# Attention and a feed-forward block in float32: attention on 128-token tiles with the mean on DVE, strips of 512 tokens, another weight conversion

## The chip, the cores and the metric

The kernel runs on one core of a Trainium2 chip. A core has engines that run side by side, each working through its own queue in order: TensorE (PE) for matrix products and transposes, with a second row PEld for loading its stationary operand; VectorE (DVE), ScalarE (ACT) and GpSimd (POOL) for elementwise work; and SyncE (SP), which here issues data transfers (DMAs). TensorE writes its results to PSUM; DVE and ACT take them from there to SBUF, the on-chip memory. The metric is the device time of one execution in microseconds (us), as the median of several runs. A profile is one further execution, recorded by the hardware profiler.

## The reference

Two blocks follow each other. The first is linear attention with a normalization per head, over 8 batches, 8 heads, 576 tokens and 64 features per head, in float32:

```python
kv = np.einsum('bhsd,bhse->bhde', k, v)
out = np.einsum('bhsd,bhde->bhse', q, kv)
rms = np.sqrt(np.mean(out * out, axis=-1, keepdims=True) + 1e-06)
attn = out / rms * g_norm
# x: (B, H, S, D) -> (B*S, H*D), 4608 tokens of 512 features
h = x @ w_in              # 512 -> 2048
r = np.maximum(h, 0.0)
out = (r * r) @ w_out     # 2048 -> 512
```

The two weights arrive as float64, which no engine here computes in. The kernel gets their bits as 64-bit integers and makes float32 of them on the chip. All products are in float32.

## The kernel before, in words

**Attention** runs in 32 units of one batch and two heads (128 features). The 576 tokens of a batch lie as 96 partitions by 6 places. `transpose_q` (L175) brings q's features onto partitions with six transposes of 96 tokens, into two PSUM tiles, copied by DVE and ACT. `key_value` (L188) forms the 128x128 product of k and v in six products, copies the two diagonal blocks (one per head) into a zeroed matrix `kvd`, and issues the loads of the unit three further on. `query` (L202) multiplies: `kvd` is stationary, q transposed streams in two halves of 288 tokens, so the result `x_ps` has features on partitions. ACT squares it. `root` (L213) gets the mean over a head's features, which now lies across partitions, by another product with a block-diagonal matrix `mean_w` of 1/64; then ACT's square root, DVE's reciprocal and a Newton step on DVE and POOL follow, all on 128x288 elements. `normalize` (L232) multiplies `x_ps` by the result and by `g_col` and writes x, already transposed, into `xT`.

**Feed-forward** runs in 12 strips of 384 tokens. `up` (L277) computes 128 of the 2048 inner features for the strip in four products of 384 columns, ACT applies the maximum with zero, DVE squares. `down` (L293) computes 128 tokens by 512 features in 16 products of 512 columns, issued in four parts; DVE or ACT copies the result and SP stores it. A strip has 16 up and 12 down steps.

**Weights** come in 32 pieces of 128x512 (16 of `w_in`, then 16 of `w_out`) through three buffers `raw`. `convert` (L112) splits each word: DVE isolates and clamps the exponent (L119, L123), ACT scales it (L126), DVE joins the sign (L127), masks the upper mantissa (L132), ACT scales that (L136), DVE adds the lower word (L137), and POOL multiplies the two parts (L140). Then the next piece's load is issued.

**The order** is written out by hand: the program's order is each engine's order. Before the first strip come the five slices of each of batch 0's four units, with a piece converted after every second slice up to eight. In strip 0, each step is preceded by one piece (later two), followed by as many slices of later units' attention as the token count asks for. Loads, weight pieces and stores all go through SP's queue in program order; only the first three units' q and the small `g_col` go through ACT's.

Of the kernel before, what the change touches and what calls it, by code (L numbers as in the profile page):

```python
# [14 lines left out]
ALU = mybir.AluOpType  # L15


@with_exitstack
def kernel(
# [27 lines left out]
    TP = S // C  # L47
    HC, HS = C // 2, S // 2
    PAIR = 2 * S  # tokens in one tile of x: two batches
    STRIP = 384  # L50
    NG = STRIP // P
    N_STRIP = n_tok // STRIP
    N_UNIT = B * NP
    AHEAD = 3  # units whose q, k, v are on chip or on their way
    OQ = 4  # pieces that the second product of 128 tokens is issued in
    N_RAW = 3
# [4 lines left out]
    qkv_pool = ctx.enter_context(tc.tile_pool(name="qkv", bufs=AHEAD))  # L61
    qt_pool = ctx.enter_context(tc.tile_pool(name="qt", bufs=3))
    xt_pool = ctx.enter_context(tc.tile_pool(name="xt", bufs=2))
    asb_pool = ctx.enter_context(tc.tile_pool(name="asb", bufs=2))
    raw_pool = ctx.enter_context(tc.tile_pool(name="raw", bufs=N_RAW))
    g_pool = ctx.enter_context(tc.tile_pool(name="g", bufs=FC + 2))
    osb_pool = ctx.enter_context(tc.tile_pool(name="osb", bufs=3))
    apsum = ctx.enter_context(tc.tile_pool(name="apsum", bufs=2, space=bass.MemoryType.PSUM))
    xpsum = ctx.enter_context(tc.tile_pool(name="xpsum", bufs=2, space=bass.MemoryType.PSUM))
# [3 lines left out]
    loaded = {}  # L73

    def load(u, eng):
        b, p = divmod(u, NP)
        hs = slice(2 * p, 2 * p + 2)
        t = {}
        # q and k are stationary operands: both heads' features lie side by side
        for n, src, e in (("q", q, eng), ("k", k, nc.sync)):  # L80
            t[n] = qkv_pool.tile([TP, C, 2, D], FP32, name=n, tag=n)
            for h in range(2):
                e.dma_start(
                    out=t[n][:, :, h, :], in_=src[b, 2 * p + h].rearrange("(sp c) d -> sp c d", c=C)
                )
        t["v"] = qkv_pool.tile([TP, 2, C, D], FP32, name="v", tag="v")
        nc.sync.dma_start(out=t["v"], in_=v[b, hs].rearrange("h (sp c) d -> sp h c d", c=C))
        loaded[u] = t

    for u in range(AHEAD):  # L90
        load(u, nc.scalar)

# [16 lines left out]

    piece_at = [0]  # L110

    def convert(n):  # L112
        while piece_at[0] < min(n, len(pieces)):
            i = piece_at[0]
            low = raw[i].bitcast(U32).rearrange("p (n two) -> p n two", two=2)[:, :, 0]
            high = raw[i].bitcast(I32).rearrange("p (n two) -> p n two", two=2)[:, :, 1]
            # 2 ** exponent with the sign; 0 below float32's normal range, inf above it
            e = asb_pool.tile([P, WN], I32, name="w_e", tag="w_e")
            nc.vector.tensor_scalar(  # L119
                out=e, in0=high, scalar1=20, scalar2=0x7FF,  # L120
                op0=ALU.logical_shift_right, op1=ALU.bitwise_and,
            )
            nc.vector.tensor_scalar(  # L123
                out=e, in0=e, scalar1=E_BIAS, scalar2=E_BIAS + 255, op0=ALU.max, op1=ALU.min
            )
            nc.scalar.activation(e, e, AF.Identity, bias=e_bias, scale=2.0**23)  # L126
            nc.vector.scalar_tensor_tensor(  # L127
                out=e, in0=high, scalar=-(2**31), in1=e, op0=ALU.bitwise_and, op1=ALU.bitwise_or
            )
            # 1 + mantissa: its upper 20 bits, then the lower 32  # L130
            top = asb_pool.tile([P, WN], I32, name="w_top", tag="w_top")
            nc.vector.tensor_scalar(  # L132
                out=top, in0=high, scalar1=0xFFFFF, scalar2=None, op0=ALU.bitwise_and
            )
            m = asb_pool.tile([P, WN], FP32, name="w_m", tag="w_m")
            nc.scalar.activation(m, top, AF.Identity, bias=one, scale=2.0**-20)  # L136
            nc.vector.scalar_tensor_tensor(  # L137
                out=m, in0=low, scalar=2.0**-52, in1=m, op0=ALU.mult, op1=ALU.add
            )
            nc.gpsimd.tensor_tensor(out=pieces[i][1], in0=m, in1=e.bitcast(FP32), op=ALU.mult)  # L140
            load_piece()
            piece_at[0] += 1

    for i in range(N_RAW):
        load_piece()
# [8 lines left out]
    E_BIAS = 1023 - 127  # L154
    e_bias = const.tile([P, 1], FP32, name="e_bias")
    nc.vector.memset(e_bias, -E_BIAS * 2.0**23)
    one = const.tile([P, 1], FP32, name="one")
    nc.vector.memset(one, 1.0)
    eps_t = const.tile([P, 1], FP32, name="eps_t")
    nc.vector.memset(eps_t, EPS)  # L160
    # block-diagonal 1/D: the mean over a head's features, on all its partitions
    mean_w = const.tile([P, P], FP32, name="mean_w")
    nc.vector.memset(mean_w, 0.0)
    nc.vector.memset(mean_w[0:D, 0:D], 1.0 / D)
    nc.vector.memset(mean_w[D:P, D:P], 1.0 / D)
    kvd = []
    for i in range(3):
        t = const.tile([P, P], FP32, name=f"kvd{i}")
        nc.vector.memset(t, 0.0)
        kvd.append(t)  # L170

# [1 line left out]
    qT, x_ps, sq, rms, xt = {}, {}, {}, {}, {}  # L173

    def transpose_q(u):  # L175
        t = qt_pool.tile([P, S], FP32, name="qT", tag="qT")
        qT[u] = t
        by_place = t.rearrange("p (sp c) -> p c sp", c=C)
        for i in range(2):
            ps = apsum.tile([P, HC, TP], FP32, name="t_ps", tag="at")  # L180
            for j in range(HC):
                nc.tensor.transpose(  # L182
                    ps[:, j, :], loaded[u]["q"][:, i * HC + j].rearrange("p h d -> p (h d)"), ident[0:TP, 0:TP]
                )
            cp = nc.scalar.copy if i else nc.vector.tensor_copy
            cp(by_place[:, i * HC : (i + 1) * HC, :], ps)  # L186

    def key_value(u):  # L188
        t = loaded.pop(u)
        ps = apsum.tile([P, P], FP32, name="kv_ps", tag="at")  # L190
        for c in range(C):
            nc.tensor.matmul(  # L192
                ps, lhsT=t["k"][:, c].rearrange("p h d -> p (h d)"), rhs=t["v"][:, :, c, :],
                start=(c == 0), stop=(c == C - 1),
            )
        d = kvd[u % len(kvd)]
        nc.scalar.copy(d[0:D, 0:D], ps[0:D, 0:D])
        nc.vector.tensor_copy(d[D:P, D:P], ps[D:P, D:P])
        if u + AHEAD < N_UNIT:
            load(u + AHEAD, nc.sync)  # L200

    def query(u):  # L202
        for i in range(2):
            ps = xpsum.tile([P, HS], FP32, name="x_ps", tag="x")
            nc.tensor.matmul(  # L205
                ps, lhsT=kvd[u % len(kvd)], rhs=qT[u][:, ts(i, HS)], start=True, stop=True
            )
            s = asb_pool.tile([P, HS], FP32, name="sq", tag="sq")
            nc.scalar.activation(s, ps, AF.Square)  # L209
            x_ps[u, i], sq[u, i] = ps, s  # L210
        del qT[u]

    def root(u):  # L213
        for i in range(2):
            ps = apsum.tile([P, HS], FP32, name="s_ps", tag="at")
            nc.tensor.matmul(ps, lhsT=mean_w, rhs=sq.pop((u, i)), start=True, stop=True)  # L216
            r = asb_pool.tile([P, HS], FP32, name="r_rms", tag="r_rms")
            nc.scalar.activation(r, ps, AF.Sqrt, bias=eps_t)  # L218
            nc.vector.reciprocal(r, r)  # L219
# [6 lines left out]
            nc.gpsimd.tensor_scalar(  # L226
                out=c, in0=c, scalar1=-0.5, scalar2=1.5, op0=ALU.mult, op1=ALU.add
            )
            nc.gpsimd.tensor_tensor(out=r, in0=r, in1=c, op=ALU.mult)  # L229
            rms[u, i] = r  # L230

    def normalize(u):  # L232
# [120 lines left out]
```

## Time and profile before

| quantity | value |
|---|---|
| median of 3 runs | 1269.7 us (1269.4 to 1270.31) |
| span of the profiled execution | 1268.2 us |
| TensorE busy (matmul) | 1150.5 us, 91% |
| weight load (PEld) | 639.3 us, 50% |
| DVE busy | 434.2 us, 34% |
| ACT busy | 230.9 us, 18% |
| POOL busy | 182.1 us, 14% |
| mean granted TensorE clock | 0.946 |
| moved by DMA | 55.14 MB, 43 GB/s over the span |

The span runs from the first to the last instruction of the core; the runs' time has a little more around it. Busy time counts an engine's instructions, overlapping ones once. The granted clock is the share of TensorE's full speed that the throttle let through. A group of instructions is given as line, engine, operation, output and inputs, shape and count, then busy time in us, mean ns of one, and the idle time of its engine just before, with what ended it. In a timeline a row gives start and length in us. A float32 matrix product leaves two matmul records in the trace, a transpose one.

### The profile page before, as it was taken

How to read it: one execution, taken by the hardware profiler on the slowest of the kernel's cores; microseconds unless marked ns; L12 is line 12 of the kernel's file. 1: busy time of each engine (PE TensorE's matmuls, PEld its weight loads, DVE VectorE, ACT ScalarE, POOL GpSimd, SP SyncE). 2: the span in 40 equal slices, each digit the busy share in tenths (PEclk: the TensorE clock that was granted, in tenths of full speed). 3: DMA queues.
4: the chain of work that ended last, by engine and by line, in shares of the span. 5: the costliest groups of instructions: out<-in, count | busy, mean ns of one | idle time of the engine just before them, and what ended most of it. 6: DMA issues, size and time to landing. Idle time of an engine off the chain costs nothing.

```text
span 1268.2 us, 9232 instructions
## 1 busy us (share of the span) xinstructions
PE 1150.5 (91%) x3520; PEld 639.3 (50%) x3520; DVE 434.2 (34%) x641; ACT 230.9 (18%) x462; POOL 182.1 (14%) x230
## 2 busy tenths in 40 slices
PE   4456645799999999999999999999999999999998
PEld 3244322356456456455465465465465565454553
DVE  3667776433233234124133233143142232220110
ACT  2323323212012112012021021021021121020110
POOL 1333232211111111101011111111011111100000
PEclk8557768899999999999999999999999999999999
DMA  8332423111111111011110111110010000000000
GB/s 215 113 106 84 127 83 111 36 45 38 36 37 28 45 37 29 26 37 28 36 42 23 44 37 29 45 32 23 35 28 9 17 1 9 17 0 17 9 0 25
DMA packets 92429, 55.14 MB, mean 43 GB/s; under 512 B 77536, under 2 KB 83680, under 8 KB 92384
## 3 DMA queue, kind: packets, MB, share of 16 engines
q1 hardware_dynamic: 88672, 53.66, 14.6%
q10 hardware_dynamic: 3712, 0.89, 0.3%
q8 instruction: 28, 0.46, 0.2%
q14 instruction: 17, 0.14, 0.0%
HBM read 45.09 MB, written 9.44 MB: 43 GB/s over the span
## 4 chain that ended last, share of the span: by engine, by line
PE 83%; DVE 10%; ACT 4%; issue 1%; POOL 1%; DMA 1%; ACTq 0%
PE o_ps L298 38%; PE h_ps L281 36%; PE kv_ps L192 3%; PE x_ps L205 2%; PE s_ps L216 2%; DVE w_e L119 2%; ACT w_e L126 2%; ACT w_m L136 2%; DVE w_e L127 2%; DVE w_e L123 2%; PE t_ps L182 1%; DVE r_rms L219 1%; DVE w_top L132 1%; DVE w_m L137 1%; DVE gt L288 1%
## 5 line engine op out<-in xcount | busy, mean ns | idle before, releaser
L281 PE MATMUL h_ps<-xT,w_in 128*128 128x384 f32 x1536 | 515.8, 493 | 0.0
L298 PE MATMUL o_ps<-w_out,gt 128*128 128x512 f32 x1152 | 505.5, 594 | 0.0
L281 PEld LDWEIGHTS h_ps<-xT,w_in 128*128 128x128 f32 x1536 | 294.0, 193 | 196.6 <-issue 11.0
L298 PEld LDWEIGHTS o_ps<-w_out,gt 128*128 128x128 f32 x1152 | 218.1, 191 | 255.1 <-issue 249.0
L288 DVE TENSOR_TENSOR gt<-r 128x384 f32<-128x384 f32 x192 | 109.5, 571 | 306.6 <-ACT r L286 306.6
L286 ACT ACTIVATE r<-h_ps 128x384 f32<-128x384 f32 x192 | 94.0, 489 | 424.8 <-PE h_ps L281 400.6
L225 POOL TENSOR_TENSOR newton<-newton,r_rms 128x288 f32<-128x288 f32 x64 | 54.8, 856 | 753.5 <-DVE newton L222 753.5
L219 DVE RECIPROCAL r_rms<-r_rms 128x288 f32<-128x288 f32 x64 | 124.6, 1947 | 64.3 <-ACT r_rms L218 64.3
L192 PE MATMUL kv_ps<-v,k 96*128 96x128 f32 x384 | 59.5, 315 | 42.7 <-DVE newton L222 42.5
L304 DVE COPY o_sb<-o_ps 128x512 f32<-128x512 f32 x24 | 16.6, 692 | 226.1 <-PE o_ps L298 223.1
L192 PEld LDWEIGHTS kv_ps<-v,k 96*128 96x128 f32 x384 | 57.0, 226 | 55.8 <-DVE newton L222 46.7
L216 PE MATMUL s_ps<-sq,mean_w 128*128 128x288 f32 x128 | 41.9, 452 | 32.5 <-ACT qT L186 32.0
L205 PE MATMUL x_ps<-qT,kvd 128*128 128x288 f32 x128 | 42.0, 456 | 30.5 <-DVE xT L239 30.5
L186 DVE COPY qT<-t_ps 128x288 f32<-128x288 f32 x32 | 21.3, 666 | 129.4 <-PE t_ps L182 129.4
L229 POOL TENSOR_TENSOR r_rms<-r_rms,newton 128x288 f32<-128x288 f32 x64 | 50.8, 794 | 5.3
L216 PEld LDWEIGHTS s_ps<-sq,mean_w 128*128 128x128 f32 x128 | 25.4, 205 | 50.0 <-ACT qT L186 34.9
L205 PEld LDWEIGHTS x_ps<-qT,kvd 128*128 128x128 f32 x128 | 26.3, 211 | 46.5 <-DVE xT L239 32.6
L209 ACT ACTIVATE sq<-x_ps 128x288 f32<-128x288 f32 x64 | 25.8, 410 | 103.2 <-PE x_ps L205 101.4
L218 ACT ACTIVATE r_rms<-s_ps,eps_t 128x288 f32<-128x288 f32 x64 | 31.2, 501 | 63.3 <-PE s_ps L216 62.6
L126 ACT ACTIVATE w_e<-w_e,e_bias 128x512 int32<-128x512 int32 x32 | 23.1, 721 | 82.4 <-DVE w_e L123 82.4
L140 POOL TENSOR_TENSOR w_in<-w_m,w_e 128x512 f32<-128x512 f32 x16 | 22.2, 1389 | 83.8 <-DVE w_m L137 83.8
L304 ACT COPY o_sb<-o_ps 128x512 f32<-128x512 f32 x12 | 7.0, 587 | 143.3 <-PE o_ps L298 136.8
(30 smaller groups left out, 330.4 us busy)
## 6 DMA issues: line engine op xcount, KB each, us to landing
k<-in_k_dram SPq DMA_DIRECT2D x64, 144.0 KB, 3.4
v<-in_v_dram SPq DMA_DIRECT2D x32, 288.0 KB, 3.7
out_dram<-o_sb SPq DMA_DIRECT2D x36, 256.0 KB, 2.0
q<-in_q_dram SPq DMA_DIRECT2D x58, 144.0 KB, 3.1
raw<-in_moe_w_in_dram SPq DMA_DIRECT2D x16, 512.0 KB, 3.6
raw<-in_moe_w_out_dram SPq DMA_DIRECT2D x16, 512.0 KB, 3.3
q<-in_q_dram ACTq DMA_DIRECT2D x6, 144.0 KB, 6.1
g_col<-in_g_norm_dram ACTq DMA_DIRECT2D x2, 0.2 KB, 3.6
```

The lines of the kernel that those rows point to most:

```text
L126: nc.scalar.activation(e, e, AF.Identity, bias=e_bias, scale=2.0**23)
L192: nc.tensor.matmul(ps, lhsT=t["k"][:, c].rearrange("p h d -> p (h d)"), rhs=t["v"][:, :, c, :], start=(c == 0), stop=(c == C - 1),)
L205: nc.tensor.matmul(ps, lhsT=kvd[u % len(kvd)], rhs=qT[u][:, ts(i, HS)], start=True, stop=True)
L216: nc.tensor.matmul(ps, lhsT=mean_w, rhs=sq.pop((u, i)), start=True, stop=True)
L218: nc.scalar.activation(r, ps, AF.Sqrt, bias=eps_t)
L219: nc.vector.reciprocal(r, r)
L225: nc.gpsimd.tensor_tensor(out=c, in0=c, in1=r, op=ALU.mult)
L229: nc.gpsimd.tensor_tensor(out=r, in0=r, in1=c, op=ALU.mult)
L281: nc.tensor.matmul(ps, lhsT=w_in[:, kc, ts(fc, P)], rhs=xt[m][:, kc, t0 : t0 + STRIP], start=(kc == 0), stop=(kc == NP - 1),)
L286: nc.scalar.activation(r, ps, AF.Relu)
L288: nc.vector.tensor_tensor(out=t, in0=r, in1=r, op=ALU.mult)
L298: nc.tensor.matmul(o_ps[0], lhsT=gt[fc][:, ts(g, P)], rhs=w_out[:, fc, :], start=(fc == 0), stop=(fc == FC - 1),)
```

## The change

All three parts are rewritten.

Attention puts tokens on partitions. A batch's 576 tokens are four chunks of 128 and a rest of 64; the rests of two batches form one tile together, so there are nine tiles of 128 tokens per two batches, 36 in all. k, v and q of a unit are loaded by five DMAs for the chunks and three for the rest, all from SP. `transposed_query` has four transposes of 128 tokens and one ACT copy (for odd batches one transpose and one DVE copy more, for the rest tile). `key_value` has five products, and POOL clears the two off-diagonal blocks of a fresh `kvd`. `query` works on one tile of 128 tokens and all 512 features: q transposed is stationary, `kvd` streams, four products (eight of half height for a rest tile). The mean is now along the free dimension: ACT squares, DVE sums by head, and square root, reciprocal and Newton step work on 128x8 elements, all on DVE but the root. DVE scales into `x_n`; `features` transposes the tile on TensorE, and ACT copies with `g_col` into `xT`.

The strips have 512 tokens, four tiles: nine strips of 16 up and 16 down steps. Strip s has its own `xT` tile. A list of slices is worked off evenly over a strip's steps but the last three, up to what the next strip needs.

The conversion clamps the upper word as a float32 (ACT's absolute value, DVE's maximum and minimum), shifts and masks it, joins sign and top exponent bit, and adds the lower word's top bits as an integer: two ACT and four DVE operations, none on POOL. Before strip 0, two pieces are converted; in it, `NP + 2 + 3 * i // 2` up to step i.

The diff, cut to its core:

```diff
-    C = 6  # token s of a batch sits at partition s // C, place s % C
-    STRIP = 384
+    C = S // P
+    REST = S - C * P
+    PAIR = 2 * C + 1
+    NT = 4
+    STRIP = NT * P
...
+        for n, src in (("k", k), ("v", v), ("q", q)):
+            whole = src[b, hs, 0 : C * P].rearrange("h (sp c) d -> sp h c d", c=C)
...
+            nc.sync.dma_start(
+                out=rest[n, b // 2, p][half], in_=src[b, hs, C * P : S].rearrange("h s d -> s h d")
+            )
...
+            nc.scalar.activation(c, high_f, AF.Abs)
             nc.vector.tensor_scalar(
+                out=c, in0=c, scalar1=LEAST, scalar2=MOST, op0=ALU.max, op1=ALU.min
+            )
             nc.vector.tensor_scalar(
+                out=ci, in0=ci, scalar1=3, scalar2=0x3FFFFFFF,
+                op0=ALU.logical_shift_left, op1=ALU.bitwise_and,
+            )
             nc.vector.scalar_tensor_tensor(
+                out=dest, in0=high, scalar=-(2**30), in1=ci, op0=ALU.bitwise_and, op1=ALU.bitwise_or
+            )
+            nc.scalar.activation(r, low, AF.Copy, scale=2.0**-29)
+            nc.vector.tensor_tensor(out=dest, in0=dest, in1=r, op=ALU.add)
...
-            nc.gpsimd.tensor_tensor(out=pieces[i][1], in0=m, in1=e.bitcast(FP32), op=ALU.mult)
...
+    def query(n):
+        m, c = divmod(n, PAIR)
+        ps = apsum.tile([P, d_model], FP32, name="x_ps", tag="at")
...
+                nc.tensor.matmul(o, lhsT=qT[b, p][:, c_b, :], rhs=kvd[b, p], start=True, stop=True)
+        nc.scalar.activation(sq, ps, AF.Square)
+        nc.vector.reduce_sum(out=ms, in_=by_head(sq), axis=AX.X)
+        nc.vector.tensor_scalar(out=ms, in0=ms, scalar1=1.0 / D, scalar2=EPS, op0=ALU.mult, op1=ALU.add)
+        nc.scalar.activation(r, ms, AF.Sqrt)
+        nc.vector.reciprocal(r, r)
+        nc.vector.scalar_tensor_tensor(out=t, in0=ms, scalar=-0.5, in1=r, op0=ALU.mult, op1=ALU.mult)
+        nc.vector.tensor_tensor(out=t, in0=t, in1=r, op=ALU.mult)
+        nc.vector.scalar_tensor_tensor(out=r, in0=t, scalar=1.5, in1=r, op0=ALU.add, op1=ALU.mult)
+        nc.vector.tensor_tensor(
+            out=by_head(x_n[n]), in0=by_head(ps), in1=r.unsqueeze(2).to_broadcast([P, H, D]), op=ALU.mult
+        )
+    def features(n):
+        for p in range(NP):
+            nc.tensor.transpose(ps[:, p, :], t[:, ts(p, P)], ident)
+        nc.scalar.activation(xt[s][:, :, ts(i, P)], ps, AF.Copy, scale=g_col)
...
+    for i in range(ready[0]):
+        attend(i + 1)
+        convert(i // 2 - 5)
     for s in range(N_STRIP):
+        attend(ready[s])
...
+            if s == 0:
+                convert(NP + 2 + 3 * i // 2)
             fn(*a)
+            attend(ready[s] + (goal - ready[s]) * (i + 1) // (len(steps) - 3))
```

More of the change, by code (lines that the diff above doesn't have):

```diff
@@ L75, in load @@
-    def load(u, eng):
-        b, p = divmod(u, NP)
+    main, rest = {}, {}
+    def load(b, p):
         hs = slice(2 * p, 2 * p + 2)
[L78 to L88, printed above, removed]
@@ L90 @@
-    for u in range(AHEAD):
-        load(u, nc.scalar)
+        half = slice(REST * (b % 2), REST * (b % 2 + 1))
+        for n, src in (("k", k), ("v", v), ("q", q)):
+            whole = src[b, hs, 0 : C * P].rearrange("h (sp c) d -> sp h c d", c=C)
+            if n == "v":
+                t = qkv_pool.tile([P, 2, C, D], FP32, name=n, tag=n)
+                nc.sync.dma_start(out=t, in_=whole)
+            else:
+                t = qkv_pool.tile([P, C, 2, D], FP32, name=n, tag=n)
+                for h in range(2):
+                    nc.sync.dma_start(out=t[:, :, h, :], in_=whole[:, h])
+            main[n, b, p] = t
+            if b % 2 == 0:
+                rest[n, b // 2, p] = rest_pool.tile([P, 2, D], FP32, name=f"{n}_rest", tag=f"{n}_rest")
+            nc.sync.dma_start(
+                out=rest[n, b // 2, p][half], in_=src[b, hs, C * P : S].rearrange("h s d -> s h d")
+            )
@@ L94, with load_next @@
+    units = [(b, p) for b in range(B) for p in range(NP)]
+    to_load = iter(units)
+    def load_next():
+        u = next(to_load, None)
+        if u is not None:
+            load(*u)
+    for _ in range(3):
+        load_next()
     w_in = wpool.tile([P, NP, d_ff], FP32, name="w_in")
@@ L114, in convert @@
             i = piece_at[0]
+            words = raw[i].bitcast(I32).rearrange("p (n two) -> p n two", two=2)
             low = raw[i].bitcast(U32).rearrange("p (n two) -> p n two", two=2)[:, :, 0]
-            high = raw[i].bitcast(I32).rearrange("p (n two) -> p n two", two=2)[:, :, 1]
-            e = asb_pool.tile([P, WN], I32, name="w_e", tag="w_e")
+            high = words[:, :, 1]
+            high_f = raw[i].bitcast(FP32).rearrange("p (n two) -> p n two", two=2)[:, :, 1]
+            dest = pieces[i][1].bitcast(I32)
@@ L135, in convert @@
[L135 to L140, printed above, removed]
+            r = wtmp.tile([P, WN], I32, name="w_r", tag="w_r")
+            nc.scalar.activation(r, low, AF.Copy, scale=2.0**-29)
@@ L166 @@
[L166 to L186, printed above, removed]
@@ L188, in key_value, with transposed_query @@
-    def key_value(u):
-        t = loaded.pop(u)
+    qT, kvd, x_n, xt = {}, {}, {}, {}
+    flat = lambda t: t.rearrange("p h d -> p (h d)")
+    def transposed_query(b, p):
+        t = main.pop(("q", b, p))
+        ps = apsum.tile([P, C, P], FP32, name="t_ps", tag="at")
+        for c in range(C):
+            nc.tensor.transpose(ps[:, c, :], flat(t[:, c]), ident)
+        qT[b, p] = qt_pool.tile([P, C, P], FP32, name="qT", tag="qT")
+        nc.scalar.copy(qT[b, p], ps)
+        if b % 2:
+            t = rest.pop(("q", b // 2, p))
+            ps = apsum.tile([P, P], FP32, name="tr_ps", tag="at")
+            nc.tensor.transpose(ps, flat(t), ident)
+            qT["rest", b // 2, p] = qt_pool.tile([P, P], FP32, name="qT_rest", tag="qT_rest")
+            nc.vector.tensor_copy(qT["rest", b // 2, p], ps)
@@ L213, in root @@
[L213 to L219, printed above, removed]
-            c = asb_pool.tile([P, HS], FP32, name="newton", tag="newton")
-            nc.vector.scalar_tensor_tensor(
-                out=c, in0=ps, scalar=EPS, in1=r, op0=ALU.add, op1=ALU.mult
-            )
-            nc.gpsimd.tensor_tensor(out=c, in0=c, in1=r, op=ALU.mult)
[L226 to L230, printed above, removed]
@@ new lines, in features @@
+    def features(n):
+        s, i = divmod(n, NT)
+        t = x_n.pop(n)
+        if s not in xt:
+            xt[s] = xt_pool.tile([P, NP, STRIP], FP32, name="xT", tag="xT")
+        ps = apsum.tile([P, NP, P], FP32, name="xt_ps", tag="at")
+        for p in range(NP):
+            nc.tensor.transpose(ps[:, p, :], t[:, ts(p, P)], ident)
+        nc.scalar.activation(xt[s][:, :, ts(i, P)], ps, AF.Copy, scale=g_col)
+    slices, ready = [], {}
+    for b in range(B):
+        for p in range(NP):
+            slices += [(transposed_query, (b, p)), (key_value, (b, p))]
+        first = b // 2 * PAIR + (C if b % 2 else 0)
+        ns = list(range(first, first + C + b % 2))
+        for i, n in enumerate(ns + [None]):
+            if n is not None:
+                slices.append((query, (n,)))
+            if i > 0:
+                slices.append((features, (ns[i - 1],)))
+                if ns[i - 1] % NT == NT - 1:
+                    ready[ns[i - 1] // NT] = len(slices)
@@ new lines, with attend, out_rows @@
+    slice_at = [0]
+    def attend(n):
+        while slice_at[0] < min(n, len(slices)):
+            fn, a = slices[slice_at[0]]
+            fn(*a)
+            slice_at[0] += 1
+    def out_rows(n):
+        m, c = divmod(n, PAIR)
+        if c == C:
+            return [
+                (slice(REST * h, REST * (h + 1)), out[(2 * m + h) * S + C * P : (2 * m + h + 1) * S, :])
+                for h in range(2)
+            ]
+        b, c_b = (2 * m, c) if c < C else (2 * m + 1, c - C - 1)
+        return [(slice(0, P), out[b * S : b * S + C * P, :].rearrange("(sp c) e -> c sp e", c=C)[c_b])]
```

162 lines of the change are left out of this document (54 added, 108 removed).

## The prediction

> **What bounds the kernel now.** I read the page's totals first, then busy time and granted clock by stages, then which engine ended the idle time of TensorE.
>
> ```profile
> span 1268.2 us, 9232 instructions
> 0.00:245.00 245.00, 131.06 (x395) 82.42 (x396) 158.18 (x246) 72.62 (x128) 74.74 (x80) 0.72 0.39 113
> 245.00:1100.00 855.00, 855.00 (x2682) 472.28 (x2680) 254.31 (x357) 141.41 (x300) 107.40 (x150) 1.00 0.11 30
> 1100.00:1268.20 168.20, 164.48 (x447) 84.55 (x445) 21.71 (x39) 16.88 (x34) 0.00 (x0) 1.00 0.03 11
> 1264.51 0.69 DVE L304 COPY o_sb<-o_ps 128x512 f32<-128x512 f32 x1 [26.78 <-PE o_ps L298]
> ```
>
> The columns of the stages are: stage, its length, busy time of PE, PEld, DVE, ACT, POOL, granted clock, DMA share, GB/s. From 245 us on, TensorE is busy all the time at clock 1.00; its last product ends shortly before 1264.5, and copy and store take the last 3.7 us. In the first 245 us it is busy for 131 us only, at clock 0.72, while DVE is busy for 158. So there are two kernels here: a start paced by something else, and a long stretch in which only the amount of TensorE work counts.
>
> What paces the start is in the last column of these groups (idle time, and who ended it):
>
> ```profile
> L192 PE MATMUL kv_ps<-v,k 96*128 96x128 f32 x384 | 59.5, 315 | 42.7 <-DVE newton L222 42.5
> L205 PE MATMUL x_ps<-qT,kvd 128*128 128x288 f32 x128 | 42.0, 456 | 30.5 <-DVE xT L239 30.5
> L216 PE MATMUL s_ps<-sq,mean_w 128*128 128x288 f32 x128 | 41.9, 452 | 32.5 <-ACT qT L186 32.0
> ```
>
> These 105 us are nearly all of the 114 us in which TensorE stood idle in the first 245. Attention products wait for PSUM tiles that DVE or ACT have yet to empty, and those two are late because the weight conversion stands ahead in their queues:
>
> ```profile
> 90.60 0.42 DVE L119 TENSOR_SCALAR w_e<-raw 128x512 int32<-128x512 int32 x1
> 91.05 0.43 DVE L123 TENSOR_SCALAR w_e<-w_e 128x512 int32<-128x512 int32 x1
> 91.57 0.72 ACT L126 ACTIVATE w_e<-w_e,e_bias 128x512 int32<-128x512 int32 x1 [2.83 <-DVE w_e L123]
> 92.33 0.69 DVE L127 SCALAR_TENSOR_TENSOR w_e<-raw,w_e 128x512 int32<-128x512 int32 x1 [0.85 <-ACT w_e L126]
> 92.93 0.42 DVE L132 TENSOR_SCALAR w_top<-raw 128x512 int32<-128x512 int32 x1
> 94.14 0.69 DVE L137 SCALAR_TENSOR_TENSOR w_m<-raw,w_m 128x512 f32<-128x512 uint32 x1 [0.79 <-ACT w_m L136]
> 94.75 0.55 DVE L288 TENSOR_TENSOR gt<-r 128x384 f32<-128x384 f32 x1
> 94.91 1.51 POOL L140 TENSOR_TENSOR w_in<-w_m,w_e 128x512 f32<-128x512 f32 x1 [4.79 <-DVE w_m L137]
> 95.22 1.49 DVE L119 TENSOR_SCALAR w_e<-raw 128x512 int32<-128x512 int32 x1
> ```
>
> DVE waits twice per piece for ACT (0.85 and 0.79 us), and the next piece's first operation takes 1.49 us instead of 0.42 while POOL multiplies. One piece and one square take 4.15 us (90.60 to 94.75) + 0.47, or 5.7 with the stretched operation. There are 32 pieces.
>
> **The dense stretch: what the change does to TensorE's work.** A float32 product shows as two matmul records, a transpose as one. Two rows of the chain of waits without attention between give the price of the large products, and a stretch of the timeline that of the others (start of a group to start of the next):
>
> ```profile
> 1099.52 41.28 PE h_ps L281 x128
> 1140.80 41.20 PE o_ps L298 x96
> 456.92 0.66 PE L182 MATMUL t_ps<-ident,q 96*128 96x96 f32 x6
> 457.42 5.35 PE L281 MATMUL h_ps<-xT,w_in 128*128 128x384 f32 x16
> 462.61 1.13 PE L216 MATMUL s_ps<-sq,mean_w 128*128 128x288 f32 x4
> 463.58 5.32 PE L281 MATMUL h_ps<-xT,w_in 128*128 128x384 f32 x16
> 468.74 1.50 PE L192 MATMUL kv_ps<-v,k 96*128 96x128 f32 x12
> 470.08 5.33 PE L281 MATMUL h_ps<-xT,w_in 128*128 128x384 f32 x16
> ```
>
> An up product of 384 columns costs 41.28/64 = 0.645 us, a down product of 512 41.20/48 = 0.858, a unit's six transposes 0.50 (0.083 each), its two 288-wide products 0.97, its six key-value products 1.34 (0.223 each, 128 columns). Before: 768 x 0.645 + 576 x 0.858 + 32 units x (0.50 + 0.97 + 0.97 + 1.34 = 3.78) = 495.4 + 494.4 + 121.0 = 1110.8 us.
>
> After, the up products are 576 of 512 columns, the down product's shape: 494.4. A key-value product runs over four chunks and a rest, 160 in all: 160 x 0.223 = 35.7. The query product now streams the 128 columns of the block-diagonal matrix, the key-value product's shape: four for each of 32 tiles and eight half-height ones for each of 4 rest tiles, 160 x 0.223 = 35.7. The mean's product (32 x 0.97 = 31.0) goes. Transposes are of 128: 144 of q and 144 of the new x, at 0.083 x 128/96 = 0.110, 31.7. No row shows them; below stands 0.083 each (-8 us), above the full product's 0.223 (+33); I take the scaled one, the same instruction being the nearest row. Sum: 494.4 + 494.4 + 35.7 + 35.7 + 31.7 = 1091.9, so **18.9 us less**. The half-height products could overlap in pairs (-3.6) at best. Strips of 512 as such bring 1 us.
>
> One rule speaks against this part: the Trainium skill, "TensorE: Matmul & The Clock Gate", section "Part 4: PE-mode transpose", says that transposes don't count as activity that holds TensorE's clock up. The timeline above has a transpose group in a stretch at granted clock 1.00, without a mark on what follows; by the rule transposes would run at half clock, by the row they do not.
>
> All other engines keep slack in this stretch; DVE has 254 us of 855 now. A strip issues 15 slices of attention over 29 steps of 3.43 us (four products of 0.858), one slice in 1.9 steps. A tile's transposes come two slices after its query product, some 13 us later. Its chain on DVE, from these rows:
>
> ```profile
> L222 DVE SCALAR_TENSOR_TENSOR newton<-s_ps,r_rms 128x288 f32<-128x288 f32 x64 | 29.3, 457 | 2.2
> L219 DVE RECIPROCAL r_rms<-r_rms 128x288 f32<-128x288 f32 x64 | 124.6, 1947 | 64.3 <-ACT r_rms L218 64.3
> L197 ACT COPY kvd<-kv_ps 64x64 f32<-64x64 f32 x32 | 6.5, 205 | 100.6 <-PE kv_ps L192 100.6
> L304 DVE COPY o_sb<-o_ps 128x512 f32<-128x512 f32 x24 | 16.6, 692 | 226.1 <-PE o_ps L298 223.1
> L119 DVE TENSOR_SCALAR w_e<-raw 128x512 int32<-128x512 int32 x32 | 26.4, 824 | 0.1
> L123 DVE TENSOR_SCALAR w_e<-w_e 128x512 int32<-128x512 int32 x32 | 22.6, 707 | 1.1
> ```
>
> The 288-wide reciprocals, 125 us of DVE, go. From 457 ns for 288 columns and 690 for 512 (L127) an operation has 0.16 us fixed. Reduction and scaling of 512 columns 0.69 each, five operations on 8 columns 0.16 each (the reciprocal's 8 x 6.8 ns adds 0.05), a square root at most 0.2 with 0.13 of handing over (0.85 waited for 0.72 of ACT, above): **2.5 us per tile**. Bounds: 1.6, if the eight-column ones were free, and 4.1, if each took a 288-wide 0.46. Both stay far below 13, so I cost it at nothing here; uncovered, it would be paid once per tile.
>
> **The start, which holds most of the gain.** Strip 0 now needs only the four tiles of batch 0 and two converted pieces in front; 26 pieces follow among the 16 up steps, 4 in the next two steps. New prices: max/min and shift/and as L119 and L123 without POOL, 0.45 each start to start; the bitwise join 0.60 as L127 to L132; the integer addition, not in the trace, between 0.47 (L288, 384 columns) and 1.5 (L140 on POOL), taken as the join's 0.60, being a 512-wide two-input DVE operation. **2.1 us per piece**; ACT's two operations (0.7 each at most) read raw words and have two buffers, so they run ahead. With max/min and shift at the means of L119 and L123 in the groups above, 0.82 and 0.71, POOL's influence included, it would be 2.7.
>
> For the loads:
>
> ```profile
> 8.17 1.20 PE L182 MATMUL t_ps<-ident,q 96*128 96x96 f32 x6 [8.17 <-DMA q<-in_q_dram]
> 9.63 2.93 PE L192 MATMUL kv_ps<-v,k 96*128 96x128 f32 x12 [0.27 <-DVE qT L186]
> 23.10 0.62 SPq L87 DMA_DIRECT2D v<-in_v_dram  x1
> 23.17 1.28 ACT L218 ACT_TABLE_LOAD   x1
> 23.90 0.35 SPq L107 DMA_DIRECT2D raw<-in_moe_w_in_dram  x1
> 24.35 1.25 SPq L83 DMA_DIRECT2D q<-in_q_dram  x2
> v<-in_v_dram SPq DMA_DIRECT2D x32, 288.0 KB, 3.7
> raw<-in_moe_w_in_dram SPq DMA_DIRECT2D x16, 512.0 KB, 3.6
> 0.00:20.00 20.00, 11.07 (x46) 9.36 (x47) 3.54 (x15) 4.23 (x8) 0.70 (x6) 1.00 0.90 239
> ```
>
> A unit becomes eight issues on SP (three for the rest tokens; ACT's queue no longer helps) of 0.62: 5 us. Three units and three raw pieces are out at 0.7 + 15 + 1 = 17 us, the fourth unit at 22, landed at 25.5. Its transposes and key-value products, at the start's slow prices, end at 28.7; the first query runs at 29, its square ends at 31.6, the square root's table load adds 1.3. Four tiles at 2.5 us, with two pieces between, and two pieces more, put DVE at 31.7 + 1.3 + 10 + 4 x 2.1 = **51.5 us**, when up 0 has its weights.
>
> From there to the last piece DVE has 28 x 2.1 = 59, sixteen squares of 512 columns at 0.60 (0.47 + 128 columns at the 1.04 ns of the two widths above) = 10, and attention: eight copies of 0.25 and two tile chains, 7. That is 76; TensorE has some 74 in it (16 x 3.43 up, 3 x 3.43 down, 9.3 attention), so the two are near each other, and DVE sets the pace. Raw pieces have three buffers: a load must land 3.6 us after its buffer comes free, with about two pieces (4.2 us) and a square to spare; each of four unit loads that SP issues in between takes 5 us and eats that. I put 2.5 us on each: 10, between 0 and 20. So the last piece is ready at 51.5 + 76 + 10 = 137.5 us, and the last quarter of the first down tile waits for it.
>
> By then TensorE has done 11.6 (batch 0 at full clock: 32 transposes, 36 small products) + 54.9 + 10.3 + 9.3 = 86.1 us of 1091.9. **Sum:** 137.5 + 1005.8 + 3.7 = 1147.0 us of span. The profiled span of before, 1268.2, is 1.5 under the median of its runs, 1269.7; with that, **1148 us**: 19 us from TensorE's work, 102 from the start (now 1268.2 - 3.7 - 1110.8 = 153.7 us lost there, then 51.4).
>
> **The rivals.**
>
> Raw pieces don't come in time. Between 51.5 and 137.5 us 28 pieces (14.7 MB) and four units (3.5 MB) must land, 212 GB/s; the first 20 us show 239 at a DMA share of 0.90. Against it: pieces are long rows, units 256 bytes. With every unit load costing its whole 5 us and two pieces late besides, +20: 1168. Chance 0.20.
>
> DVE's operations keep the lengths that they now have beside POOL, or the addition is slow: 28 x 0.65 = +18, 1166. For it: 1.49 in the row above; against: POOL keeps only two small clears per unit. 0.07.
>
> The conversion doesn't get shorter, because ACT, which also holds the up steps' activations, hands each piece over late: with today's 5.7 less the square's 0.47, so 5.2 per piece, 28 x (5.2 - 2.1) = +87, about 1235. For it: both waits of today; against: two buffers. 0.07.
>
> Transposes run at half clock: 31.7 us more, 1180. This is the rule of Part 4 of the Trainium skill's page on TensorE; no row here bears it out. 0.03.
>
> The normalization of a tile comes out from under its cover: TensorE, in order, stands at the transposes of x until DVE has written it, and behind them stand the up and down products. Below 13 us of chain it costs nothing, above it the excess for each of 32 tiles. The gain of 121 us is eaten from 3.8 us each, a chain of 17 us, seven times my sum; then slower, some 1275 or more. 0.05.
>
> **How the numbers follow.** The forecast has 0.52, with 1133 to 1160 as its own range (no stall on raw pieces and paired half products; or twice the stall). Better than that, 0.05, by cheaper transposes. The rivals have 0.20, 0.07, 0.07, 0.03, 0.05; no change 0.01, were the two gains both hidden. The range 1130 to 1190 holds the forecast and the rivals from 1166 to 1180 and leaves out some 0.18. Faster by more than 0.2%, about what this kernel's runs can tell from nothing: 0.94; within it 0.01; slower 0.05.
>
> **What would show it.** Right: TensorE busy all the time at clock 1.00 from about 140 us on; up products 0.858 us; a query tile 0.89 us; pieces on DVE every 2.1 us plus a square, with no wait for ACT; the last conversion near 137 us. Wrong: conversion operations that wait for a DMA or for ACT, or last beyond 160 us; TensorE idle before the transposes of x in the dense stretch; a clock under 1.00 there.

## The result, and the profile after

The changed kernel takes 1158.12 us (median of 4 runs, 1157.05 to 1159.19) against 1269.78 us before: ratio 0.9123, 95% interval 0.911 to 0.9135, 111.7 us less. The profiled execution has a span of 1156.2 us, 1.9 us under that median; the forecast span was 1147.0.

The page of the changed kernel, with busy time and instructions of each engine, and two groups with the idle time of TensorE before them:

```profile
span 1156.2 us, 8506 instructions
PE 1115.7 (96%) x3232; PEld 545.0 (47%) x3232; DVE 272.4 (24%) x590; ACT 210.7 (18%) x400; POOL 10.5 (1%) x70
...
L307 PE MATMUL o_ps<-w_out,gt 128*128 128x512 f32 x1152 | 513.0, 598 | 6.7 <-DVE w_out L159 6.7
L290 PE MATMUL h_ps<-xT,w_in 128*128 128x512 f32 x1152 | 508.3, 596 | 1.5 <-ACT xT L251 0.8
```

Its stages (length, busy time of PE, PEld, DVE, ACT, POOL, granted clock, DMA share, GB/s):

```profile
40.00:60.00 20.00, 12.93 (x37) 6.20 (x36) 17.79 (x39) 12.55 (x23) 0.00 (x0) 0.83 0.53 159
53.80:139.00 85.20, 78.35 (x240) 38.11 (x240) 76.90 (x151) 45.66 (x83) 1.70 (x8) 0.97 0.65 202
139.00:160.00 21.00, 20.98 (x58) 10.42 (x59) 3.49 (x9) 2.67 (x5) 0.00 (x0) 0.87 0.06 24
139.00:1156.20 1017.20, 1013.21 (x2882) 488.41 (x2882) 177.32 (x392) 148.26 (x285) 5.51 (x38) 1.00 0.11 28
```

The dense stretch begins at 139 us instead of 245; until then TensorE is idle for 139.0 - 102.5 = 36.5 us instead of 114 (its 102.5 us are 1115.7 less the 1013.2 of the last row). After 139 us it stands still only for the last 4 us, in which the last tile is copied and stored.

DVE's timeline shows one piece of the conversion and what TensorE waits for at the end of the start:

```profile
51.44 0.42 DVE L143 TENSOR_SCALAR w_c<-w_c 128x512 f32<-128x512 f32 x1
51.90 0.43 DVE L148 TENSOR_SCALAR w_c<-w_c 128x512 int32<-128x512 int32 x1
52.36 0.69 DVE L153 SCALAR_TENSOR_TENSOR w_in<-raw,w_c 128x512 int32<-128x512 int32 x1
53.19 0.69 DVE L159 CUSTOM_DVE_ANT_0 w_in<-w_in,w_r 128x1024 uint16<-128x1024 uint16 x1
53.80 0.42 DVE L143 TENSOR_SCALAR w_c<-w_c 128x512 f32<-128x512 f32 x1
...
138.28 0.69 DVE L159 CUSTOM_DVE_ANT_0 w_out<-w_out,w_r 128x1024 uint16<-128x1024 uint16 x1
```

A piece takes 53.80 - 51.44 = 2.36 us with no wait for ACT in it. From 53.8 us, when up 0 has its four pieces, to 139 DVE works practically without a gap (its waits there are 1.0 us for ACT's first operation on a piece and 0.5 us for the square root); its last conversion starts at 138.28 and TensorE goes on at 139.03.

TensorE's timeline, first in the start, then in the dense stretch (start, length; the difference of two starts is what a group costs):

```profile
48.54 4.63 PE L290 MATMUL h_ps<-xT,w_in 128*128 128x512 f32 x6 [0.78 <-ACT xT L251]
...
123.14 1.05 PE L223 MATMUL x_ps<-kvd,qT 128*128 128x128 f32 x8
124.03 3.60 PE L307 MATMUL o_ps<-w_out,gt 128*128 128x512 f32 x8
...
139.03 7.18 PE L307 MATMUL o_ps<-w_out,gt 128*128 128x512 f32 x10 [3.01 <-DVE w_out L159]
146.04 1.05 PE L223 MATMUL x_ps<-kvd,qT 128*128 128x128 f32 x8
...
384.74 1.09 PE L218 MATMUL x_ps<-kvd,qT_rest 128*64 128x128 f32 x16
385.77 3.70 PE L307 MATMUL o_ps<-w_out,gt 128*128 128x512 f32 x8
389.31 1.05 PE L223 MATMUL x_ps<-kvd,qT 128*128 128x128 f32 x8
...
572.10 0.60 PE L250 MATMUL xt_ps<-ident,x_n 128*128 128x128 f32 x4
572.53 7.03 PE L290 MATMUL h_ps<-xT,w_in 128*128 128x512 f32 x16
...
594.12 1.05 PE L197 MATMUL kv_ps<-v,k 128*128 128x128 f32 x8
595.11 0.49 PE L198 MATMUL kv_ps<-v_rest,k_rest 64*128 64x128 f32 x2
595.52 3.70 PE L290 MATMUL h_ps<-xT,w_in 128*128 128x512 f32 x8
599.06 0.60 PE L182 MATMUL t_ps<-ident,q 128*128 128x128 f32 x4
```

Four query products cost 0.89 us (123.14 to 124.03) and four transposes 0.43. Eight half-height query products cost 1.03 (384.74 to 385.77), 0.13 each instead of 0.223: they overlap. The key-value products do not fit: the four of 128 rows take 0.99 instead of 0.89, the one of 64 rows takes 0.41 instead of 0.22, and the four up products behind it take 3.54 (595.52 to 599.06) instead of 4 x 0.858 = 3.43. So a unit costs 1.40 instead of 1.12 by its own rows, and 1.50 with the 0.10 behind it: 0.385 us more than five products at 0.223. Units of even batches take the lower 64 partitions of the rest tile, those of odd batches the upper; both take 0.41 to 0.42.

### The profile page after: what moved, and what is told of

Its sections match the earlier page's. It is cut to its first block, busy times and chain, and to the rows that moved or that the text cites. A ratio compares the mean times of both kernels' runs of the same rounds, so it can differ in the third digit from the quotient of the medians.

```text
span 1156.2 us, 8506 instructions
## 1 busy us (share of the span) xinstructions
PE 1115.7 (96%) x3232; PEld 545.0 (47%) x3232; DVE 272.4 (24%) x590; ACT 210.7 (18%) x400; POOL 10.5 (1%) x70
## 4 chain that ended last, share of the span: by engine, by line
PE 93%; SPq 2%; DVE 2%; DMA 1%; ACT 1%; issue 0%; DVEq 0%; ACTq 0%
PE h_ps L290 43%; PE o_ps L307 42%; PE kv_ps L197 2%; PE x_ps L223 2%; PE xt_ps L250 1%; PE t_ps L182 1%; SPq L91 1%; PE kv_ps L198 1%; SPq L95 1%; DMA raw<-in_moe_w_out_dram 0%; DMA q<-in_q_dram 0%; PE x_ps L218 0%; DVE w_c L148 0%; SPq L86 0%; DVE w_out L153 0%
## 5 line engine op out<-in xcount | busy, mean ns | idle before, releaser
L290 PE MATMUL h_ps<-xT,w_in 128*128 128x512 f32 x1152 | 508.3, 596 | 1.5 <-ACT xT L251 0.8
L290 PEld LDWEIGHTS h_ps<-xT,w_in 128*128 128x128 f32 x1152 | 215.4, 191 | 255.4 <-issue 248.2
L296 DVE TENSOR_TENSOR gt<-r 128x512 f32<-128x512 f32 x144 | 99.6, 691 | 414.1 <-ACT r L294 414.1
L294 ACT ACTIVATE r<-h_ps 128x512 f32<-128x512 f32 x144 | 85.8, 596 | 365.5 <-PE h_ps L290 365.4
L228 DVE TENSOR_REDUCE ms<-sq 128x8 f32<-128x512 f32 x36 | 24.6, 684 | 157.3 <-ACT sq L226 157.3
L197 PEld LDWEIGHTS kv_ps<-v,k 128*128 128x128 f32 x256 | 35.9, 205 | 13.4 <-issue 13.4
L251 ACT ACTIVATE xT<-xt_ps,g_col 128x512 f32<-128x512 f32 x36 | 24.6, 683 | 93.2 <-PE xt_ps L250 93.2
L223 PEld LDWEIGHTS x_ps<-kvd,qT 128*128 128x128 f32 x256 | 33.6, 194 | 13.6 <-issue 13.6
L197 PE MATMUL kv_ps<-v,k 128*128 128x128 f32 x256 | 36.3, 289 | 0.0
L223 PE MATMUL x_ps<-kvd,qT 128*128 128x128 f32 x256 | 34.1, 277 | 0.0
```

The source lines that it names most:

```text
L197: nc.tensor.matmul(ps, lhsT=flat(tk[:, c]), rhs=tv[:, :, c, :], start=(c == 0), stop=False)
L223: nc.tensor.matmul(o, lhsT=qT[b, p][:, c_b, :], rhs=kvd[b, p], start=True, stop=True)
L228: nc.vector.reduce_sum(out=ms, in_=by_head(sq), axis=AX.X)
L251: nc.scalar.activation(xt[s][:, :, ts(i, P)], ps, AF.Copy, scale=g_col)
L290: nc.tensor.matmul(ps, lhsT=w_in[:, kc, ts(fc, P)], rhs=xt[s][:, kc, :], start=(kc == 0), stop=(kc == NP - 1))
L294: nc.scalar.activation(r, ps, AF.Relu)
```

## The experiments

My theory: the start is set by DVE's time per converted piece, the dense stretch by the sum of TensorE's products, and what the sum missed is the key-value product over the 64 rest tokens. The rivals are in the expectations.

### The old conversion in the changed kernel

```diff
-            nc.scalar.activation(c, high_f, AF.Abs)
-            ... (max/min, shift/and, join, lower word, integer addition)
+            nc.vector.tensor_scalar(out=e, in0=high, scalar1=20, scalar2=0x7FF, ...)
+            ... (the ten lines of the kernel before, POOL's product at the end)
```

> Edit: the changed kernel with the conversion of before (five DVE operations, two of ACT between them, one of POOL). Theory: the length of a piece on DVE's path sets the start; 5.2 us instead of 2.36 for 28 to 32 pieces is 80 to 91 us more: about 1240 us. Rival: the new order of attention (two pieces ahead of strip 0 instead of eight) freed the start; then under 1200.

Measured: 1244.14 us (ratio to before 0.9799, 0.9784 to 0.9813), 86.0 us above the changed kernel. DVE's timeline in strip 0:

```profile
103.74 0.42 DVE L138 TENSOR_SCALAR w_e<-raw 128x512 int32<-128x512 int32 x1
104.20 1.37 DVE L142 TENSOR_SCALAR w_e<-w_e 128x512 int32<-128x512 int32 x1
106.41 0.69 DVE L146 SCALAR_TENSOR_TENSOR w_e<-raw,w_e 128x512 int32<-128x512 int32 x1 [0.85 <-ACT w_e L145]
107.02 0.42 DVE L151 TENSOR_SCALAR w_top<-raw 128x512 int32<-128x512 int32 x1
108.23 0.69 DVE L156 SCALAR_TENSOR_TENSOR w_m<-raw,w_m 128x512 f32<-128x512 uint32 x1 [0.79 <-ACT w_m L155]
108.84 0.69 DVE L301 TENSOR_TENSOR gt<-r 128x512 f32<-128x512 f32 x1
```

A piece takes 5.10 us (103.74 to 108.84); (5.10 - 2.36) x 32 = 88. The theory's sum holds; without the shorter conversion the new attention with its strips is worth 25 us.

### The new conversion in the kernel before

```diff
-            nc.vector.tensor_scalar(out=e, in0=high, scalar1=20, scalar2=0x7FF, ...)
-            ... (the ten lines of before)
+            nc.scalar.activation(c, high_f, AF.Abs)
+            ... (the conversion of the change)
```

> Edit: the kernel before with the new conversion alone. Theory: the same 2.8 us per piece, 32 pieces, 90 us less: about 1180 us, TensorE's 1111 us of work unchanged. Rival: in the old attention the reciprocals of 1.95 us and the Newton steps on POOL hold TensorE up by themselves, and most of the start's loss stays: over 1225.

Measured: 1196.6 us (0.9427, 0.9411 to 0.9443), 73 us less than before, not 90, and nearer to the theory than to the rival. The stages show the start at 155 us instead of 245:

```profile
0.00:155.00 155.00, 105.54 (x350) 68.85 (x351) 118.87 (x198) 65.94 (x125) 26.97 (x42) 0.94 0.66 172
155.00:1194.40 1039.40, 1034.25 (x3171) 564.20 (x3169) 286.04 (x410) 159.52 (x337) 111.59 (x156) 1.00 0.10 27
```

and what still holds TensorE up there is the old attention on DVE, as the rival has it, for 34 us (waits up to 200 us; in total, times, longest):

```profile
PE kv_ps L188 <- DVE newton L218: 19.1, 6, 9.3
PE x_ps L201 <- DVE xT L235: 15.1, 5, 4.4
```

Conversion alone 73 us, attention and strips alone 25.6, all 111.7: the two help each other by 13.

### The rest product over 128 rows

```diff
+            k_pad[h, p] = restc.tile([P, 2, D], FP32, name=f"k_pad{h}{p}")
+            nc.vector.memset(k_pad[h, p], 0.0)
...
+            if n == "k":
+                rest[n, b // 2, p] = k_pad[b % 2, p]
...
         nc.tensor.matmul(
-            ps, lhsT=flat(rest["k", b // 2, p][half]), rhs=rest["v", b // 2, p][half], start=False, stop=True
+            ps, lhsT=flat(k_pad[b % 2, p]), rhs=v_pad[p], start=False, stop=True
```

> Edit: the rest's key-value product contracts over all 128 rows; k's rest lies in a tile of its own per batch parity whose other 64 rows are zero. Theory: the change of height costs. In the changed kernel the four chunk products and the 64-row product of a unit take 1.40 us (594.12 to 595.52), five products of the chunk's price would be 1.12; with one height throughout they become that, 32 x 0.28 = 9 us less: 1149 us. Rival: the 0.41 us of the rest product comes from its operands (tiles and loads of their own); then it stays and the time stays at 1158.

Measured: 1149.43 us (0.9051, 0.9039 to 0.9064), 8.7 us less. In TensorE's timeline the unit is at 1.12 us, with both groups at their price (0.90 and 0.22):

```profile
590.18 1.05 PE L209 MATMUL kv_ps<-v,k 128*128 128x128 f32 x8
591.08 0.39 PE L210 MATMUL kv_ps<-v_pad,k_pad 128*128 128x128 f32 x2
591.30 3.60 PE L302 MATMUL h_ps<-xT,w_in 128*128 128x512 f32 x8
```

The rest's operands still come from tiles and loads of their own, so these were not the cost: the number of rows was. That 32 x 0.28 came so near to the 8.7 is luck. Eight of the 32 units lie before 139 us, where DVE sets the pace; the other 24 save 0.385 each, 9.2 us, and TensorE's dense stretch (139.67 to 1143.66 us, 1004.0) is shorter by just that than the changed kernel's (139.03 to 1152.23, 1013.2).

### The rest product twice

```diff
+        nc.tensor.matmul(ps, lhsT=flat(rest["k", ...][half]), rhs=rest["v", ...][half], start=False, stop=False)
         nc.tensor.matmul(ps, lhsT=flat(rest["k", ...][half]), rhs=rest["v", ...][half], start=False, stop=True)
```

> Edit: the changed kernel issues the 64-row rest product of k and v twice in a row (the rest counts twice in the output). Theory: the change of height between neighbours costs, so the second of two alike adds only a chunk's 0.22 us: 32 x 0.22 = 7 us, 1165. Rival: each 64-row product costs 0.4 us by itself: 32 x 0.41 = 13 us, 1171.

Measured: 1163.85 us (0.9168, 0.9153 to 0.9183), 5.7 us more than the changed kernel. TensorE's timeline:

```profile
598.65 1.05 PE L197 MATMUL kv_ps<-v,k 128*128 128x128 f32 x8
599.63 0.48 PE L198 MATMUL kv_ps<-v_rest,k_rest 64*128 64x128 f32 x2
599.96 0.38 PE L201 MATMUL kv_ps<-v_rest,k_rest 64*128 64x128 f32 x2
600.27 3.70 PE L293 MATMUL h_ps<-xT,w_in 128*128 128x512 f32 x8
```

Both together take 0.64 us (599.63 to 600.27); one took 0.41. So a further one costs 0.23 us, as much as a 128-row product, and what was missed, 0.28 us in the unit's rows and 0.10 behind them, is paid once for going to 64 rows and back. That the time grew by 5.7 us and not by 7 fits the units that count in full: 24 x 0.23 = 5.5. The Trainium skill, "TensorE: Matmul & The Clock Gate", section "Why this matters for your kernels", says that a single product over 32 rows takes as long as one over 128; the second product here, over 64 rows, agrees with 0.23 against 0.22 us.

### More buffers for raw pieces

```diff
-    raw_pool = ...(name="raw", bufs=3)
+    raw_pool = ...(name="raw", bufs=5)
-    for _ in range(3): load_piece()
+    for _ in range(5): load_piece()
```

> Edit: five instead of three buffers for raw weight pieces. The prediction put 10 us on raw pieces that land late behind unit loads; if they cost that, up to 10 us go: 1148 us. Rival, from the trace of the changed kernel: DVE works without a gap from 53.8 to 139 us, so the pieces are never late for it; then the time stays within 2 us of 1158.

Measured: 1159.56 us (0.9135, 0.9123 to 0.9148), nothing gained. The edit also moved the start: two more raw loads stand ahead of the fourth unit's loads, whose transposes begin at 30.07 us instead of 27.34, and the first up step begins at 52.80 instead of 48.54. ACT's waits for raw pieces (28 us in the changed kernel) turn into waits for DVE, and TensorE's last piece comes at 141.76 instead of 139.03 us:

```profile
ACT w_c L142 <- DVE w_out L153: 10.6, 10, 1.8
ACT w_c L142 <- DVE w_in L153: 7.4, 7, 1.8
PE o_ps L307 <- DVE w_out L159: 6.4, 3, 3.9
```

From the first up step to the last piece it takes 89.0 us instead of 90.5, so the buffers brought 1.5 us at most, and the later start took more than that. The 10 us that the prediction put on late pieces were not there.

### Three pieces where DVE waits

```diff
-        convert(i // 2 - 5)
+        convert(0 if i < 5 else 3 if i < 15 else 4)
```

> Edit: three pieces are converted before the fourth unit's slices, where DVE waits (22 to 31 us), instead of two behind the third and fourth tile, and the fourth behind batch 0's last slice. Theory: DVE sets the pace up to 139 us, so 3 x 2.36 = 7 us go: 1151 us, and the first up step begins near 45 us instead of 48.5. Rival: TensorE is as tight as DVE there (busy 20 of 20 us from 60 to 120) or the loads move along, and the gain is under 3 us.

Measured: 1153.11 us (0.9084, 0.9072 to 0.9097), 5.0 us less, between the two expectations. The first up step began at 47.84 us, 0.7 earlier and not 3.5. The tile chain could not start earlier, because q of the fourth unit landed no sooner: its transposes begin at 27.48 us, 27.34 in the changed kernel. What is saved behind them is the one piece that stood ahead of the last tile, 2.36 us, and part of that is lost again, with TensorE's granted clock from 27 to 48 us at 0.66 instead of 0.83; why it was lower stays open. TensorE's last piece came at 136.13 us, 2.9 earlier. The versions below, with the same early pieces, began their up steps at 45.5, 48.4 and 47.5.

### How long the tile's chain may be

```diff
+        if n >= PAIR:
+            for _ in range(8):   # and 24
+                nc.vector.reduce_sum(out=more, in_=by_head(sq), axis=AX.X)
         x_n[n] = xn_pool.tile([P, d_model], FP32, name="x_n", tag="x_n")
```

> Edit: eight more reductions (0.61 us each from start to start, results unused) in each tile's chain from tile 9 on, 27 tiles. Theory: TensorE comes to a tile's transposes 13 us after its query product, so a chain of 2.7 + 4.9 us is still covered: no change, 1158 us. Rival: any growth of the chain is paid, 27 x 4.9 = 132 us: 1290.

> Edit: 24 more reductions, 14.6 us. Chain 17 us and more against a cover of 13: TensorE stands idle ahead of the transposes of x, about 5 us for each of 27 tiles, 135 us more (60 to 190): some 1290 us. If the cover is larger than I think, no change.

Measured: with eight 1157.37 us (0.9116, 0.9103 to 0.913), the changed kernel's time. With 24 1255.4 us in one run, 97 us more, 3.6 for each of 27 tiles; less than my 135, inside the 60 to 190. The group in that run:

```profile
L254 PE MATMUL xt_ps<-ident,x_n 128*128 128x128 f32 x100 | 20.2, 338 | 58.9 <-DVE x_n L243 58.9
```

TensorE stands for 59 us between 300 and 1200 us ahead of the transposes of x, and its granted clock, 0.988 for the changed kernel, is 0.956. The idle time is not the whole cost:

```profile
716.33 1.12 PE L254 MATMUL xt_ps<-ident,x_n 128*128 128x128 f32 x4 [2.86 <-DVE x_n L243]
717.24 8.06 PE L311 MATMUL o_ps<-w_out,gt 128*128 128x512 f32 x16
725.13 1.05 PE L223 MATMUL x_ps<-kvd,qT 128*128 128x128 f32 x8
```

Behind this wait of 2.86 us the clock is 0.60 (716.33 to 720 us), four transposes take 0.91 us instead of 0.43, and eight down products 7.89 instead of 6.87. Over the span, idle time ahead of these transposes grew by 65 us (9.7 to 74.4) and busy time by 32 (1115.7 to 1148.0), which make the 97.

So the cover exists, and at a chain of 17 us the change's gain is nearly gone. But 13 us is only its lower end. In the changed kernel, from tile 9 on, 11.6 to 64 us pass from a tile's first query product to its first transpose: the transposes come two slices after the query product for the first and the last tile of a batch and three slices after it for the others, and strips with fewer slices spread them over more steps. So TensorE waits at 13 of the 27 tiles, 2.9 to 7.7 us each, and not 5 us at every one.

### Taken together

Three versions put the readings to use: the padded rest product, the early pieces and strip 0's squares on ACT; then five raw buffers with two pieces per step; then five buffers, of which two are filled behind the loads of the start, with the old pieces per step.

```diff
+        if s == 0:
+            nc.scalar.activation(t, r, AF.Square)     # all three
+        if i == 8:
+            load_piece(); load_piece()                # the third
```

> Edit: the padded rest product, the early pieces, and strip 0's squares on ACT instead of DVE. If the first two readings hold and take 9 and 7 us, and DVE, relieved of 16 x 0.60 us in strip 0, no longer sets the pace, TensorE does from about 45 us on: the waits before the first down tile's last products (7 us) go, 1133 to 1140 us. Rival: ACT, with 10 us more, becomes the pace: not under 1142.

> Edit: the kernel with padded rest, early pieces and squares on ACT, and besides five raw buffers and two pieces per step in strip 0. In that kernel DVE waits 13.5 us for pieces that land late and TensorE 5.6 us, at clock 0.67, for the last pieces. Theory: once DVE has slack, the raw buffers are the pace, which they were not in the changed kernel; with five, TensorE is dense from 46 us on: some 8 to 10 us less, 1134 us. Rival: the DMA's throughput sets the landing, and more buffers bring under 3 us: 1140 or more.

> Edit: the kernel with padded rest, early pieces and squares on ACT, with five raw buffers of which two are first filled behind the loads of the start, and the old count of pieces per step. The version with five buffers filled at once and two pieces per step began its up steps at 48.4 instead of 45.5 us, behind two more raw loads, and let TensorE wait 6.7 us for a copy behind the pieces on DVE; neither holds here. If late raw pieces are what is left, DVE's 13.5 us of waits go and with them TensorE's for the last pieces: 1135 us. If the DVE's own work is: 1141 or more.

Measured: 1143.18 us (0.9003, 0.8989 to 0.9016), 1145.48 (0.9028, 0.9014 to 0.9041) and 1135.69 (0.8942, 0.893 to 0.8954). The first missed its 1133 to 1140. Its rival's bound of 1142 fits, but not the reason, ACT's work: with less to do DVE waited for pieces, and ACT in turn for the raw loads. The second missed its 1134: two more raw loads ahead of the fourth unit's put its first up step at 48.4 us instead of 45.5, and TensorE waited 6.7 us for a copy behind the pieces on DVE. The third met 1135. The wait that decides, in the first and in the second:

```profile
DVE w_c L155 <- ACT w_c L154: 13.5, 6, 4.0
ACT w_c L154 <- DMA raw<-in_moe_w_out_dram: 12.2, 6, 4.1
```

```profile
PE x_ps L230 <- DVE kvd L218: 6.7, 1, 6.7
```

In the third version these waits of DVE are 5.8 us instead of 13.5, and TensorE's before the down products 1.3 instead of the first version's 5.6 (6.7 in the changed kernel):

```profile
L322 PE MATMUL o_ps<-w_out,gt 128*128 128x512 f32 x1152 | 507.6, 593 | 1.3 <-DVE w_out L171 1.3
```

So two more buffers, filled behind the loads of the start, bring 7.5 us over the first version, where DVE no longer sets the pace alone. The second version differs from the third in two things, the early filling and the two pieces per step; which of them cost how much was not separated. The third version is 22 us faster than the changed kernel.

## Why the prediction was right, and where its terms were off

Forecast 1148, measured 1158, inside the range of 1130 to 1190 and the likeliest case's own 1133 to 1160. Gained were 111.7 us where 121 were forecast.

**What bounds each stretch** held. TensorE is dense from 139 us (140 forecast), and the two exchange runs show the conversion as the start's pace.

**The end of the start**, 137.5 us, was 139.0, but by luck: its errors cancel. A piece was put at 2.1 us and took 2.36: the join and the addition after it stand 0.83 us apart (52.36 to 53.19), not 0.60. The excess is 28 x 0.25 = 7 us of the 9.2 by which the 85.2 us from there to the last piece exceed the 76 forecast. The 10 us for late raw pieces were not there: ACT did wait for them, DVE did not, because it needed 3.0 us per piece with squares and attention (85.2 us for 28), and it was already the later of the two. The first up step began at 48.5 us with the pieces that were there, and the last piece of its four was ready at 53.8; forecast was 51.5 for that.

**TensorE's work** was the term that missed, and the traces of the dense stretch say by how much. Large products 0.858, transposes 0.110 and query products 0.223 us were as priced. The half-height ones overlap, which the prediction had only as its best case: eight cost 1.03 us, and 1.23 with 0.10 at either edge, instead of 1.78. The key-value rest product, priced like a chunk's, cost 0.385 us more per unit, 0.10 of it in the product behind it; over the 24 units after 139 us that is 9.2 us. That the prediction counted "128 columns" and not the rows was the mistake. The rows of before could not warn of it: they have 96-row products between 128-row ones (eight up products from 463.58 to 468.74 in 5.16 us, six key-value products to 470.08 in 1.34), at no extra cost, and none of 64 rows.

**The sum.** The span is 9.2 us over the forecast. The last piece was 1.5 late, but three of the four products that I had behind it were already done, -2.6. After 139 us, 24 units pay 0.385, +9.2; three rest tiles 0.55 less each, -1.7. The clock was at 0.87 from 139 to 160 us: ten records took 7.0 us (139.03 to 146.04) instead of 4.3, +2.7. The tail was 0.3 longer. These make 9.4, the 9.2 within the rounding of the rows.

**The transposes at half clock** did not show: four take 0.43 to 0.44 us and the stretch is at clock 1.00. By the Trainium skill's "Part 4: PE-mode transpose" of the page "TensorE: Matmul & The Clock Gate" transposes don't hold the clock up; these traces, with at most five in a row between long products, neither need the rule nor can test it on a stretch of transposes alone.

**The rival on the other side** named the right mechanism with a place and a point: a chain of 17 us was to eat the gain, and the run with 24 more reductions stands at 1255. How it is paid was not right: the excess over 13 us is not paid at each tile but at 13 of 27, and a wait costs more than its length, by the slower products behind it. At the real chain, 2.7 us on DVE, it is nothing.

## What to carry to other kernels

Price the start and the dense stretch apart: in the one a queue's time per piece counts, with its round trips, in the other the sum of products. When a product's shape is new, compare all three of its sizes with a row, the contracted one too; zero rows can be cheaper than a change to 64 rows and back. Where two resources are close (here DVE and the raw loads), relieving the slower one shows the other, and a wait on an engine that feeds a later one is no cost yet.

## What the runs showed of the hardware that was not expected

A 64-row product between 128-row ones costs 0.385 us more than a 128-row one: about 0.10 ahead of it, 0.19 in it and 0.10 in the product behind it; two of them in a row pay that once. In the kernel before, 96-row products between 128-row ones cost nothing extra (0.223 each).

Query products that write 64 partitions each, in turn the lower and the upper half of a tile, overlap: eight take 1.03 us (384.74 to 385.77), while four that write all 128 take 0.89.

A wait of TensorE in a dense stretch cost more than its length: behind one of 2.86 us the granted clock was 0.60 for 3.7 us, and twelve products and transposes took 1.5 us longer.

The integer addition of two int32 tiles runs as a DVE operation on 128x1024 uint16, at 0.69 us for 512 words, the length of a two-input operation on 512 float32; the next operation can follow after 0.61, but it itself began 0.83 behind the join that writes its operand.
